# Two more unit boundaries with shared column tiles in a four-layer convolution and FFN kernel

## The chip, the cores and the metric

The kernel runs on one core of one Trainium2 chip, in one launch. The metric is device time in microseconds (us), lower being better. The kernel before was timed in three runs: 342.99, 343.20 and 343.58 us, median 343.2. One more execution was recorded by the hardware profiler; its own time was 343.52 us.

## What is computed

The reference applies two kinds of block in turn, A, B, A, B, to a sequence of 2048 tokens of 512 channels, all tensors in bf16. Block A (`_A_ref`) shifts k by a four-tap filter, multiplies it by v, convolves the product along the sequence with a filter as long as the sequence (by FFT), adds a direct term and multiplies by the normalised q. Block B is a gated feed-forward network (FFN) with 1792 hidden columns:

```python
x = A_q
x = x + _A_ref(_layernorm(x), A_k, A_v, A_shift_k, A_ssm_k, A_ssm_D)
x = x + _B_ref(_layernorm(x), B_w_gate, B_w_up, B_w_down)
x = x + _A_ref(_layernorm(x), A_k, A_v, A_shift_k, A_ssm_k, A_ssm_D)
x = x + _B_ref(_layernorm(x), B_w_gate, B_w_up, B_w_down)

def _B_ref(x, w_gate, w_up, w_down):
    return (silu(x @ w_gate) * (x @ w_up)) @ w_down
```

The convolution in A depends on k, v and the two filters only, so both A layers use the same one; the kernel computes it once.

## The kernel before

**Tiling.** The sequence is cut into four blocks of 512 tokens (index c), each held as 128 partitions by 4 rows. A block is worked on in two halves (index h) of two rows, that is 256 tokens. A *unit* is (layer, c, h): the FFN of one layer for one half. There are 16 units, and the order of `UNITS` (L946) is block by block, layer 0 then layer 1, half 0 then half 1: ... (1,1,0), (1,1,1), (0,2,0), (0,2,1), (1,2,0), (1,2,1), ..., (1,3,1).

**The convolution.** Each block's k·v and filter piece are transformed by matmuls with cosine and sine tables (lines 443, 470 and 544, all of which issue through `mm` at L323 or at L470), multiplied on VectorE (`product`, L639), and transformed back (`inverse`, L693, or for block 0 `inverse_half`, L795). ScalarE empties the matmuls' PSUM banks at L431 and L703. This work for block c+2 is spread among the FFN units of block c. The shift filter is done by 128-column matmuls with diagonal weights (`shift_mul`, L509) or, for blocks 2 and 3, by scaled copies on ScalarE (L616) and DMA transposes.

**Before a unit.** `prologue` (L894) normalises x on VectorE or ScalarE, multiplies by the convolution's result, adds, normalises again into `z` (L879 or L874), and has a DMA on SyncE's queue (SP) transpose each of the two rows of z into a slot of `zT` (L908). There are three `zT` slots; the transposed tile is what the gate and up matmuls stream.

**A unit.** `ffn` (L1003) splits the 14 column tiles of 128 hidden columns into groups, normally of 4, 4, 4 and 2. For each group `gate_up` (L949) fills PSUM banks `pf` (four of them) with gate and up products: two column tiles of 256 tokens fill a bank of 512 columns, with four matmuls of 256 streamed columns for each tile. ScalarE turns them into `sg` (silu, L974) and `ht` (L977), VectorE multiplies the two (L979), and `down` (L982) accumulates into two `pd` banks by matmuls of 512 columns. ScalarE and VectorE add the sums to x (L1075, L1078), and in layer 1 a store on SP's queue writes the row out (L1086).

**Shared column tiles.** `SHARE` (L54) names units whose last two column tiles are computed together with the next unit's (L1023 to L1027). In such a group the streamed operand is two `zT` slots at once:

```python
lo, hi = sorted(z.slot for z in zs)
return zall.t[:, lo:hi + 1:hi - lo, kd]
```

One column tile of two units then fills a bank of 512 columns: four matmuls of 512 streamed columns where there were eight of 256. The products for the next unit are kept and used when that unit comes (`left`, L1023). A shared group can only start when the next unit's `zT` has landed. Before, three boundaries are shared, after units (1,0,1), (0,2,0) and (1,3,0).

**The last unit.** For (1,3,1) the second row's down sums are split into columns 0 to `TAIL` and `TAIL` to 512 (L986, L1016). The first part goes through VectorE (L1049) and a store on SP, the second through ScalarE (L1052) and a store on ScalarE's queue (L1055). `TAIL` is 320. The first row goes out at L1039 and L1044.

**The order of the work.** Every operation is recorded with `plan.add`. The list `ORDER` gives one rank per operation, and each engine gets its operations in the order of rank (`Plan.order`, L190). Nothing is reordered afterwards: each engine runs its list, and SP and ScalarE issue DMAs in theirs. `Plan.issue` (L220) also puts *warming* matmuls on a constant tile (L1307) where its own estimates leave TensorE idle in the first 32 us; line 228 says how many. There are 25 before the four small transposes of the filter taps (L1173), 5 between them and the first transposes of the filter (`hn`, L489), and 2 more near 22 us.

Of the kernel before, what the change touches and what calls it, by code (L numbers as in the profile page):

```python
# [32 lines left out]
X0 = 'direct'  # L33
# [5 lines left out]
XVE = "AAAAAAAA"  # L39
# [12 lines left out]
TAIL = 320  # L52
VE_D = False
SHARE = {(1, 0, 1): 2, (0, 2, 0): 2, (1, 3, 0): 2}  # L54
ORDER = [
# [85 lines left out]
class Plan:  # L141
# [78 lines left out]
    def issue(self, seq, place, when, warm_until, warm):  # L220
        t, busy = 0.0, {}
# [1119 lines left out]
```

## Time and profile before

| What | Value |
|---|---|
| Median of three runs | 343.2 us (342.99 to 343.58) |
| Profiled execution's own time | 343.52 us |
| Its span | 341.7 us |
| TensorE busy | 337.7 us, 99% of the span |
| VectorE busy | 282.4 us, 83% |
| ScalarE busy | 252.5 us, 74% |
| GpSimd busy | 37.0 us, 11% |
| Mean DMA rate | 67 GB/s |
| Granted TensorE clock, mean | 0.999 |

The span is from the core's first to its last profiled instruction. PE is TensorE's matmuls and PEld its weight loads, which overlap the matmuls; DVE is VectorE, ACT ScalarE, POOL GpSimd, SP SyncE; a trailing q (SPq, ACTq) means the engine's sequencer, which waits or issues DMAs. In rows of groups, "out<-in" are the kernel's tile names, then the partitions and columns, the count, busy time in us and the mean duration of one in ns. The matmuls are pipelined: the duration of one (379 ns at 512 columns) is longer than the distance between two starts.

### The profile page before, as it was taken

The numbers are of one execution on the slowest core, as the hardware profiler recorded it, in microseconds if no ns is written. First come the engines' busy times: TensorE is split into PE (matmuls) and PEld (weight loads), VectorE is DVE, ScalarE is ACT, GpSimd is POOL, SyncE is SP. The second block draws the span as 40 slices with busy tenths as digits, with TensorE's granted clock in tenths as the row PEclk, the third lists the DMA queues.
The fourth block names the chain that finished last, engine by engine and source line by source line (L and its number), as shares of the span: only waits on it lengthen the run. The fifth ranks groups of instructions, "written<-read, shape, count | busy, mean of one in ns | idle before, by whom it ended". The sixth has DMA issues, their size and how long they took to land.

```text
span 341.7 us, 6468 instructions
## 1 busy us (share of the span) xinstructions
PE 337.7 (99%) x2563; PEld 243.7 (71%) x2563; DVE 282.4 (83%) x478; ACT 252.5 (74%) x496; POOL 37.0 (11%) x46
## 2 busy tenths in 40 slices
PE   9999999999999999999999999999999999999996
PEld 7656868768686567868587756868685877777683
DVE  7899999999999999999999999889997533726022
ACT  6899999999978475778999973869675545545451
POOL 4010100102105100103110100101101000001000
PEclk9999999999999999999999999999999999999999
DMA  7999314050215155010100224010101110001001
GB/s 287 326 293 359 59 27 67 0 155 1 34 38 102 31 96 169 2 31 2 33 19 14 48 42 129 0 33 1 33 0 39 39 36 0 16 17 28 20 33 31
DMA packets 42088, 22.95 MB, mean 67 GB/s; under 512 B 33989, under 2 KB 39882, under 8 KB 42058
## 3 DMA queue, kind: packets, MB, share of 16 engines
q1 hardware_dynamic: 41904, 22.49, 26.0%
q8 instruction: 20, 0.33, 0.4%
q14 instruction: 10, 0.08, 0.1%
q10 hardware_dynamic: 154, 0.05, 0.1%
HBM read 12.33 MB, written 2.10 MB: 42 GB/s over the span
## 4 chain that ended last, share of the span: by engine, by line
PE 96%; ACT 3%; issue 0%; ACTq 0%
PE pf L323 57%; PE pd L994 28%; PE ps L323 6%; PE ps L470 2%; ACT H L431 1%; PE wm L1307 1%; PE pt L489 1%; ACT Yk L729 1%; ACT ks L526 0%; ACT n L874 0%; PE pt L378 0%; ACT zT L940 0%; ACT X L431 0%; ACT xc L1052 0%; PE pt L1173 0%
## 5 line engine op out<-in xcount | busy, mean ns | idle before, releaser
L323 PE MATMUL pf<-zT,wg_sb 128*128 128x256 bf16 (+1 forms) x872 | 110.3, 275 | 0.0
L323 PE MATMUL pf<-zT,wu_sb 128*128 128x256 bf16 (+1 forms) x872 | 110.0, 275 | 0.1
L994 PE MATMUL pd<-wd_sb,ht 128*128 128x512 bf16 (+1 forms) x462 | 106.2, 373 | 0.0
L323 PEld LDWEIGHTS <-wu_sb 128*128 128x128 bf16 x872 | 85.3, 98 | 18.9 <-issue 0.6
L323 PEld LDWEIGHTS <-wg_sb 128*128 128x128 bf16 x872 | 85.3, 98 | 17.4
L977 ACT CAST ht<-pf 128x512 bf16<-128x512 f32 x112 | 64.7, 589 | 23.3 <-PE pf L323 22.9
L974 ACT ACTIVATE sg<-pf 128x512 bf16<-128x512 f32 x112 | 66.3, 603 | 20.8 <-PE pf L323 17.3
L994 PEld LDWEIGHTS <-ht 128*128 128x128 bf16 x462 | 45.0, 98 | 44.1
L979 DVE TENSOR_TENSOR ht<-ht,sg 128x1024 bf16<-128x1024 bf16 (+1 forms) x61 | 38.8, 640 | 19.9 <-ACT ht L977 13.8
L826 POOL TENSOR_TENSOR rstd<-ve,nhalf 128x2 f32<-128x2 f32 x24 | 25.0, 1045 | 192.7 <-DVE ve L824 192.7
L821 DVE BATCH_NORM_STATS2 bnst<-xc 128x6 f32<-128x512 bf16 x48 | 31.8, 684 | 0.5
L1075 ACT CAST dn<-pd 128x512 bf16<-128x512 f32 x30 | 17.3, 590 | 17.5 <-PE pd L994 17.5
L431 ACT ACTIVATE X<-ps 128x512 bf16<-128x512 f32 x32 | 19.0, 607 | 10.5 <-PE ps L323 10.0
L1078 DVE TENSOR_TENSOR xc<-xc,dn 128x1024 bf16<-128x1024 bf16 x15 | 10.3, 686 | 16.8 <-ACT dn L1075 16.8
L669 DVE TENSOR_TENSOR t<-X,G 128x2048 bf16<-128x2048 bf16 x18 | 21.9, 1216 | 0.1
L665 DVE TENSOR_TENSOR t<-X,G 128x2048 bf16<-128x2048 bf16 x18 | 21.9, 1217 | 0.0
L855 POOL TENSOR_TENSOR rstd<-ve,nhalf 128x2 f32<-128x2 f32 x8 | 8.4, 1044 | 79.6 <-ACT ve L853 79.6
L679 DVE TENSOR_TENSOR Z<-Z,t 128x2048 bf16<-128x2048 bf16 x12 | 14.7, 1221 | 0.3
L677 DVE TENSOR_TENSOR t<-t,t 128x2048 bf16<-128x2048 bf16 x12 | 14.6, 1219 | 0.2
L431 ACT ACTIVATE H<-ps 128x512 bf16<-128x512 f32 x24 | 14.1, 611 | 0.0
L901 DVE TENSOR_TENSOR n<-n,Yk 128x1024 bf16<-128x1024 bf16 x15 | 10.3, 689 | 3.2 <-ACT n L874 1.9
L323 PE MATMUL ps<-hs,fwd 128*128 128x512 bf16 x40 | 12.7, 379 | 0.1
(103 smaller groups left out, 322.4 us busy)
## 6 DMA issues: line engine op xcount, KB each, us to landing
hn<-in_A_ssm_k_dram SPq DMA_DIRECT2D x4, 512.0 KB, 5.4
vt<-in_A_v_dram SPq DMA_DIRECT2D x4, 512.0 KB, 5.2
xc<-in_A_q_dram SPq DMA_DIRECT2D x4, 512.0 KB, 4.7
out_dram<-xc SPq DMA_DIRECT2D x15, 128.0 KB, 1.8
wg_sb<-in_B_w_gate_dram SPq DMA_DIRECT2D x1, 1792.0 KB
wu_sb<-in_B_w_up_dram SPq DMA_DIRECT2D x1, 1792.0 KB, 8.2
wd_sb<-in_B_w_down_dram SPq DMA_DIRECT2D x1, 1280.0 KB, 11.9
kn<-in_A_k_dram SPq DMA_DIRECT2D x1, 512.0 KB, 4.5
```

The costliest lines, as they stand in the source:

```text
L323: nc.tensor.matmul(o, lhsT=lhsT, rhs=rhs, start=(n == 0), stop=(n == len(terms) - 1))
L431: add("ACT", act(D), lambda: nc.scalar.activation(out=view(), in_=ps.t[:], func=ACT.Copy, scale=scale), r=[ps], w=[(buf, keys)], conv=conv)
L665: dve(n * D, lambda t1=t1, part=part: nc.vector.tensor_mul(out=t1.t[:], in0=x.t[:, sl, 0, :], in1=g.t[:, sl, part, :]), [(x, key(slots, (0 ...
L669: dve(n * D, lambda t2=t2, part=part: nc.vector.tensor_mul(out=t2.t[:], in0=x.t[:, sl, 1, :], in1=g.t[:, sl, 1 - part, :]), [(x, key(slots ...
L679: dve(n * D, lambda t1=t1, part=part: nc.vector.tensor_add(out=z.t[:, sl, part, :], in0=z.t[:, sl, part, :], in1=t1.t[:]), [t1], [zk], con ...
L821: add("DVE", 0.6, lambda st=st, i=i: nc.vector.bn_stats(out=st.t[:], in_=xs[c].t[:, i, :]), r=[(xs[c], (i,))], w=[st])
L826: add("POOL", pw, lambda: nc.gpsimd.tensor_tensor(out=rstd.t[:], in0=ve.t[:], in1=nhalf.t[:].to_broadcast((P, n)), op=ALU.pow), r=[ve, nha ...
L974: add("ACT", act(D), lambda ps=ps, sl=sl: nc.scalar.activation(out=sg.t[:, sl], in_=ps.t[:], func=ACT.Silu), r=[ps], w=[(sg, (b,))], due=( ...
L977: add("ACT", act(D), lambda ps=ps, sl=sl: nc.scalar.copy(out=ht.t[:, sl], in_=ps.t[:]), r=[ps], w=[(ht, (b,))], due=(us[0], at, 1.5, "a"))
L979: dve(n * m * W, lambda: nc.vector.tensor_mul(out=ht.t[:], in0=ht.t[:], in1=sg.t[:]), [sg], [ht], due=(us[0], (k + n) / NF, 0.0, "h"))
L994: nc.tensor.matmul((pds[o] if not cs.start else pds[HP]).t[:, cs], lhsT=ht.t[:, q, at, o * P:(o + 1) * P], rhs=wt["d"].t[:, ft, cs], start ...
L1075: add("ACT", act(D), lambda o=o: nc.scalar.copy(out=dn.t[:, o, :], in_=pds[o].t[:]), r=[pds[o]], w=[(dn, (o,))], due=(unit, 1.0, 3.0, "h"))
```

## The change

- `SHARE` gets two more entries: units (1,1,1) and (1,2,0). The boundary after (1,1,1) is one between blocks 1 and 2 and between layers 1 and 0. Unit (0,2,0) now takes over two shared column tiles and passes on two.
- `TAIL` goes from 320 to 384: the last row is stored as 384 columns by way of VectorE and SP and 128 by way of ScalarE.
- The count of warming matmuls in line 228 becomes 27 before the tap transposes and 3 after them; the 2 near 22 us stay.
- `ORDER` is another list. Up to about 100 us of the profiled execution each engine has its old sequence, but for three places: near 12 us ScalarE takes the squares of one row (L845) ahead of the sum of the next (L840) and not behind it, near 26.5 us one inverse matmul of block 0 (L809) stands ahead of 16 shift matmuls (L519) and not behind them, and near 82 us one multiplication at L979 stands ahead of a row's statistics (L821). From there on the sequences of TensorE, VectorE, ScalarE and SP differ in many places. On SP, stores, the loads of blocks 3 and the transposes stand in another order; at the end one L1086 store stands between the L1044 store and the L1055 store.
- A branch `X0 == "mix"` is added; `X0` is 'direct' in both kernels, so it is not taken.

The program for TensorE is 32 matmuls and 32 weight loads shorter, VectorE's has one multiplication at L979 less, and the other engines have the same operations as before.

```diff
-TAIL = 320
+TAIL = 384
-SHARE = {(1, 0, 1): 2, (0, 2, 0): 2, (1, 3, 0): 2}
+SHARE = {(1, 0, 1): 2, (0, 2, 0): 2, (1, 3, 0): 2, (1, 1, 1): 2, (1, 2, 0): 2}
 ORDER = [
...
-    97, 98, 58, 59, 99, 101, 61, 76, 22, 23, 25, 47, 33, 24, 70, 55, 54, 29, 32, 62, 42, 57, 68, 38, 63, 28, 53, 43, 44, 45, 46, 56, 65, 48, 51, 141,
+    97, 98, 58, 59, 99, 101, 61, 78, 22, 23, 25, 47, 33, 24, 70, 55, 54, 29, 32, 62, 42, 57, 68, 38, 63, 28, 53, 43, 44, 45, 46, 56, 65, 48, 51, 141,
...
-                            n = int((start - t - (0.35 if 0.0 < t < 8.0 else 0.3)) / 0.106)
+                            n = int((start - t - (0.3 if t > 8.0 else 0.5 if t > 0.0 else 0.1)) / 0.106)
...
+        elif X0 == "mix":
+            evx = spectrum("evx")
+            X[0] = spectrum("X0")
+            direct(vt[0], X[0], "pf", eng(XVE[:4]), (0, 2))
...
-        if X0 == "half":
+        if X0 in ("half", "mix"):
```

108 rows, old and new, of the table ORDER are left out of this document.

## The prediction

> **What bounds the kernel now.** I read the page first, then the busy time of each engine by stage, then the groups with their shapes kept apart, then the chain of waits, then the timeline at both ends. From the page, and from the table by stage:
>
> ```profile
> span 341.7 us, 6468 instructions
> PE 337.7 (99%) x2563; PEld 243.7 (71%) x2563; DVE 282.4 (83%) x478; ACT 252.5 (74%) x496; POOL 37.0 (11%) x46
> ```
>
> ```profile
> 0.00:6.40 6.40, 5.58 (x53) 5.17 (x54) 4.73 (x20) 3.78 (x7) 3.19 (x14) 1.00 0.71 254
> 6.40:33.00 26.60, 26.36 (x246) 16.94 (x245) 24.88 (x53) 24.88 (x53) 2.31 (x3) 1.00 1.07 331
> 33.00:165.00 132.00, 132.00 (x984) 96.14 (x983) 129.62 (x208) 111.12 (x223) 19.48 (x16) 1.00 0.27 55
> 165.00:338.70 173.70, 173.70 (x1287) 125.43 (x1284) 122.94 (x199) 112.41 (x215) 12.04 (x14) 1.00 0.12 29
> ```
>
> The columns after the stretch are its length, then busy time (and count) of PE, PEld, DVE, ACT and POOL, granted clock, DMA share, GB/s. From 33 to 338.7 us TensorE is busy for 132.00 of 132.00 and 173.70 of 173.70 us: it waits for nobody. So in nine tenths of the run a new order has no wait to remove; it can only add one. The time falls there only if TensorE's own work gets shorter. What is not solid TensorE work lies in the first 33 us and in the 3 us after its last matmul.
>
> **The shared column tiles.** How much shorter is the work? A busy row cannot say, since matmuls overlap; the chain of waits gives stretches without a gap (start, length, what):
>
> ```profile
> 285.62 10.48 PE pf L323 x96
> 296.11 6.04 PE pd L994 x28
> ```
>
> 96 gate and up matmuls of 256 columns in 10.48 us are 109.2 ns each, 28 down matmuls of 512 columns in 6.04 us are 215.7 ns each. Two of 256 cost 218.3, one of 512 costs 215.7: a pair saves 2.6 ns. That the wide form in `gate_up` costs the same as in `down` is in the groups, where both last 379 ns:
>
> ```profile
> L994 PE MATMUL pd<-wd_sb,ht 128*128 128x512 bf16 x434 | 103.0, 379 | 0.0
> L323 PE MATMUL pf<-zT,wu_sb 128*128 128x512 bf16 x24 | 6.0, 379 | 0.0
> ```
>
> A boundary shares 2 column tiles, each with gate and up, each of 4 contraction steps: 16 pairs. Two boundaries are 32 pairs, 32 x 2.6 ns = 0.08 us. The 32 weight loads that go save nothing more: they lie beside the matmuls (PEld 125.43 against PE 173.70). Nor does the DVE multiplication that goes: two of 512 columns become one of 1024 on an engine with 50 us idle in that stage. Sum so far -0.08 us, with ends 0 and -0.10 (the rounding of the two lengths).
>
> **The warming matmuls.** The first 7 us of TensorE, and eight later transposes with their follower:
>
> ```profile
> 0.76 2.82 PE L1307 MATMUL wm<-const-bfloat16-1.0 128*128 128x128 bf16 x25 [0.76 <-PEq L1325]
> 3.52 0.28 PE L1173 MATMUL pt<-ident,tapR 4*128 4x4 bf16 x4
> 3.73 0.72 PE L1307 MATMUL wm<-const-bfloat16-1.0 128*128 128x128 bf16 x5
> 4.50 1.86 PE L489 MATMUL pt<-ident,hn 128*128 128x128 bf16 x16
> 6.17 0.96 PE L378 MATMUL pt<-ident,kn 128*128 128x128 bf16 x12
> ...
> 8.48 0.39 PE L323 MATMUL ps<-dg,kTb 128*128 128x128 bf16 x4
> ...
> 18.53 0.61 PE L489 MATMUL pt<-ident,hn 128*128 128x128 bf16 x8
> 18.98 1.03 PE L470 MATMUL ps<-vt,fwd 128*128 128x512 bf16 x4
> ```
>
> 16 hn transposes take 6.17 - 4.50 = 1.67 us, 104 ns each; later, 8 take 0.45 us, 56 ns each. The array starts at half rate and changes near 6.2 us, though the granted clock reads 1.00 throughout. The change moves two warming matmuls from behind the tap transposes to ahead of them; the total stays 30. At about 107 ns each the 27 end near 3.65, so the taps start some 0.15 us after 3.52. The first hn transpose waits for its DMA, not for TensorE:
>
> ```profile
> PEld L489 <- DMA hn<-in_A_ssm_k_dram: 0.3, 1, 0.3
> ```
>
> So 4.50 stays. The later taps delay `tapF` and the 16 diagonal tiles made from it by 0.15 us. The first of these is read at 8.48 us, behind transposes and filter matmuls without a gap. I take 0. Ends: +0.15 (all of the delay on the path) and -0.77 (the half rate ends before the hn transposes: 16 x 48 ns). The trace is nearest to 0, because the same 30 matmuls start at the same 0.76. The Trainium skill, TensorE: Matmul & The Clock Gate, Part 1, says that the array's gate looks at activity in a window of some 3.4 us that runs freely, so that the change of rate moves by about 0.5 us from run to run; by that rule the edit does nothing and both kernels scatter by an estimated 0.25 us, half of that, around the same sum. The one profile shows the change once and cannot show the scatter.
>
> **The three moves before 100 us.** ScalarE's sum and square near 12 us change places: the same instructions, with TensorE unbroken behind them until 22 us. The multiplication near 82 us runs 0.6 us earlier and the statistics later, in a stretch without a TensorE wait. Price 0 each. The inverse matmul:
>
> ```profile
> 26.28 0.38 PE L323 MATMUL ps<-hs,fwd 128*128 128x512 bf16 x1
> 26.49 0.38 PE L809 MATMUL ps<-m,inv 128*128 128x512 bf16 x1
> 26.71 1.06 PE L323 MATMUL ps<-dg,kTb 128*128 128x128 bf16 x16
> 27.60 1.03 PE L809 MATMUL ps<-m,inv 128*128 128x512 bf16 x4
> ```
>
> It now follows the one at 26.49, which reads the other half of the same `m` tile and writes the same bank, so it has nothing of its own to wait for. The 16 shift matmuls move back by 0.22 us and their evacuation with them. By 27.8 us both orders have done the same work. Ends 0 and +0.22; I take 0, as three quarters of the shift work stays where it was.
>
> **The order after 100 us.** Work is only moved, and TensorE has no wait to lose, so the end on the good side is 0. For the other end I added up the rows' durations along the changed order, each engine by its list, and asked where a TensorE instruction is ready only just in time. The same sum over the order of before gives no wait after 33 us, as the profile has it. Two kinds of place are narrow. The first is a forward transform's bank:
>
> ```profile
> L431 ACT ACTIVATE X<-ps 128x512 bf16<-128x512 f32 x32 | 19.0, 607 | 10.5 <-PE ps L323 10.0
> ```
>
> The ring `pc` has two banks. The new order has, near 116 us, two transform matmuls, 8 gate matmuls (0.87), and a third transform. It stands 0.43 + 0.87 = 1.30 us behind the first; the first bank is free after 0.38 + 0.61 = 0.99 and two hand-overs. That leaves at most 0.3 us to spare, if ScalarE goes to it at once; if another 0.6 us copy stands first, TensorE stalls for 0.3 or more. The second is a `zT` tile: a shared group reads the next unit's tile before the present unit ends. For (1,2,1), before:
>
> ```profile
> 240.29 2.50 SPq L908 DMA_TRANSPOSE zT<-z  x2
> ```
>
> ```profile
> 245.02 1.91 PE L323 MATMUL pf<-zT,wu_sb 128*128 128x256 bf16 x16
> ```
>
> ```profile
> DMA to landing us min/median/max: 2.4/2.4/4.0
> ```
>
> Its second transpose is issued 1.2 us before 242.79, so near 241.6, lands near 244.0 and is wanted at 245.0: 1.0 us to spare. By my sum the new order wants it 2.2 us earlier and issues it only 1.6 us earlier: 0.5 us to spare (an estimate). The other new boundary has about 2. SP's moved stores and loads (each issue 0.3 to 0.6 us) and the load of block 3's `kTb` (some 26 us later, wanted 10 us after it lands) stand where SP otherwise waits for z. I take 0. Ends 0 and, for a landing at the largest 4.0 instead of 2.4, 1.6 - 0.5 = +1.1 us.
>
> **The tail.**
>
> ```profile
> 337.06 0.69 DVE L1039 TENSOR_TENSOR xc<-xc,pd 128x512 bf16<-128x512 bf16 x1 [2.09 <-PE pd L994]
> 337.77 0.33 SPq L1044 DMA_DIRECT2D out_dram<-xc  x1
> 338.47 0.49 DVE L1049 TENSOR_TENSOR xc<-xc,pd 128x320 bf16<-128x320 bf16 x1 [0.73 <-PE pd L994]
> 338.80 0.32 ACT L1052 CAST xc<-pd 128x192 bf16<-128x192 f32 x1 [4.56 <-PE pd L994]
> 338.99 0.33 SPq L1055 DMA_DIRECT2D out_dram<-xc  x1
> 339.15 0.38 ACTq L1055 DMA_DIRECT2D out_dram<-xc  x1
> ```
>
> ```profile
> out_dram<-xc SPq DMA_DIRECT2D x1, 80.0 KB, 1.7
> out_dram<-xc ACTq DMA_DIRECT2D x1, 48.0 KB, 1.7
> L1075 ACT CAST dn<-pd 128x512 bf16<-128x512 f32 x30 | 17.3, 590 | 17.5 <-PE pd L994 17.5
> ```
>
> Both stores take 1.7 us to land, whatever their size, so ScalarE's (339.15 + 1.7 = 340.85) ends the work, 0.16 after SP's. ScalarE's copy at 128 columns: between 0.32 at 192 and 0.59 at 512, a column is 0.85 ns, so 64 fewer are -0.05. SP's part: its four last matmuls end 4 x 64 columns later (215.7/512 = 0.42 ns a column, +0.11), and VectorE takes 64 columns more, at (0.69 - 0.49)/192 = 1.04 ns +0.07; together +0.18. New ends 340.80 and 340.87: +0.02. The store put ahead of L1055 fits the 0.88 us in which SP waits after 338.10; without that cover it would cost its 0.33 to 0.43. I take 0; ends -0.05 and +0.43.
>
> **Sum.** -0.08 + 0 + 0 + 0 + 0 = about -0.1 us on the profiled execution's 343.5 (a span of 341.7 and 1.8 around it). That execution is 0.3 above the median of the three runs, 343.2, so I put the time at 343.1. The runs differ by 0.6 us, 0.2%, which is about what a measurement tells from no change: 342.5 to 343.9 counts as the same.
>
> **The rivals.** *The half rate ends earlier.* The gap between the 25 warming matmuls and the taps (about 3.4 to 3.52) closes. If that lets the array change before 4.5 us, the 16 hn transposes save 0.77 us, TensorE has hardly a gap from there to 33 us (26.36 of 26.60 busy), and the gain lasts: 343.1 - 0.8 = 342.3. For it: the first stretch is where time is left. Against it: the gap is 0.1 us, the 0.26 us ahead of hn stays, and 30 matmuls are 30 matmuls. Chance 0.10.
>
> *TensorE waits for a shared tile.* The (1,2,1) tile lands late. It decides once the landing is 0.5 us over the median; at 4.0 us it costs 1.1: 343.1 + 1.1 = 344.2, slower. A too tight bank hand-over would add to it in steps of 0.3. For it: 4.0 is in the trace. Against it: the median equals the smallest, 2.4, so late ones are few. Chance 0.13.
>
> *Sharing saves nothing,* because the wide matmuls that read two slots run slower than `down`'s, by the 2.6 ns: 343.2. Against it: 379 ns in both rows. Chance 0.05.
>
> **How the numbers follow.** My forecast has 0.72, its own range 342.7 to 343.5 (the spread of the runs and the small ends above). Faster takes 0.10 from the first rival and 0.02 from the forecast's edge; slower 0.11 from the second and 0.01 from the edge; the rest, 0.76, is the same. The range 342.4 to 343.9 leaves out the far halves of the two outer rivals.
>
> **What would show it.** Right: PE without a gap from 33 us to the end, 856 rows each for gate and up, 40 of them wide at 379 ns; taps near 3.65, hn still near 4.5; the last two stores landing within 0.1 us of each other. Wrong: a TensorE wait behind `zT` near 242 us or behind L431 near 116; hn transposes at 56 ns; a last store that lands clearly later after TensorE's end than 2.1 us.

## The result and the profile after

The changed kernel takes 344.16 us (median of 20 executions, 343.5 to 346.31), the kernel before 343.26 us (20 executions, 342.86 to 345.06). The ratio is 1.0027, with a 95% interval of 1.0014 to 1.0039: slower by 0.9 us, 0.27%. The prediction said 343.1 us and no change, with 343.9 as its upper end; it was wrong.

The profiled execution does not show the loss in its total. Its span is 341.7 us and its own time 343.55 us, against 341.7 and 343.52 before. The page, the table by stage (stretch, then busy time and count of PE, PEld, DVE, ACT and POOL, granted clock, DMA share, GB/s) and TensorE's waits:

```profile
PE 336.9 (99%) x2531; PEld 239.2 (70%) x2531; DVE 281.9 (83%) x477; ACT 252.1 (74%) x496; POOL 38.0 (11%) x46
```

```profile
33.00:165.00 132.00, 132.00 (x982) 95.84 (x980) 128.69 (x206) 110.81 (x222) 19.72 (x16) 1.00 0.26 55
165.00:338.70 173.70, 173.16 (x1251) 121.58 (x1249) 122.84 (x199) 112.02 (x215) 12.78 (x14) 1.00 0.13 28
```

```profile
PE pf L323 <- DMA zT<-z: 0.4, 1, 0.4
PE pt L378 <- DMA kn<-in_A_k_dram: 0.2, 1, 0.2
```

Before, the stretch from 165 us on was solid, 173.70 of 173.70. Now 0.54 us are missing from it: 0.37 in the one wait that TensorE has there, behind a `zT` tile, and 0.17 at the end, as its last matmul now ends at 338.54 and not behind 338.70. The 0.37 count from the modelled end of the matmul before; by the starts of the matmuls the wait is longer, as worked out below. The timeline of after has its place, and what stands ahead of it:

```profile
162.04 0.68 DVE L979 TENSOR_TENSOR ht<-ht,sg 128x1024 bf16<-128x1024 bf16 x1
...
163.16 1.44 POOL L826 TENSOR_TENSOR rstd<-ve,nhalf 128x2 f32<-128x2 f32 x2 [6.00 <-DVE ve L824]
...
164.63 0.23 DVE L863 SCALAR_TENSOR_TENSOR nmr<-mv,rstd 128x2 f32<-128x2 f32 x2 [0.63 <-POOL rstd L826]
...
164.94 1.52 ACT L874 ACTIVATE z<-xc,nmr,rstd 128x512 bf16<-128x512 bf16 x2 [0.61 <-DVE nmr L863]
...
165.78 2.53 SPq L908 DMA_TRANSPOSE zT<-z  x2
...
169.58 0.59 PE L323 MATMUL ps<-Z,inv 128*128 128x512 bf16 x2
170.55 1.05 PE L323 MATMUL pf<-zT,wg_sb 128*128 128x256 bf16 x8 [0.37 <-DMA zT<-z]
```

The matmul at 170.55 is the first of unit (1,1,1). It reads its own tile, in a group that is not shared. TensorE has nothing else left and would have started at 170.02, after the two inverse matmuls. So 0.53 us are lost. The same stretch before:

```profile
162.70 0.72 POOL L826 TENSOR_TENSOR rstd<-ve,nhalf 128x2 f32<-128x2 f32 x1 [5.27 <-DVE ve L824]
163.45 0.16 DVE L863 SCALAR_TENSOR_TENSOR nmr<-mv,rstd 128x2 f32<-128x2 f32 x1
163.66 0.69 DVE L979 TENSOR_TENSOR ht<-ht,sg 128x1024 bf16<-128x1024 bf16 x1
163.96 1.56 ACT L874 ACTIVATE z<-xc,nmr,rstd 128x512 bf16<-128x512 bf16 x2
164.84 2.50 SPq L908 DMA_TRANSPOSE zT<-z  x2
...
169.82 1.91 PE L323 MATMUL pf<-zT,wu_sb 128*128 128x256 bf16 x16
```

Before, the statistics came ahead of the multiplication L979, and one L826 gave one L863. After, L979 stands ahead, two L826 run one behind the other (163.16 to 164.59), and both L863 wait for the second, although the z in question needs only the first, which ended at 163.94. The second transpose was issued at 166.08 before and at 167.03 after, 0.95 us later; TensorE wants it at 169.82 and 170.02, 0.20 later. With the typical 2.44 us from issue to landing that leaves 1.30 us to spare before and 0.55 after. It should still have done. But the transposes did not take 2.44 us. From before and from after, the two of this tile:

```profile
DMA to landing us min/median/max: 2.4/2.8/3.2
```

```profile
DMA to landing us min/median/max: 2.7/3.1/3.5
```

The second took 3.19 us before, so it landed at 169.27, still 0.55 ahead of its use. It took 3.47 after and landed at 170.50, 0.48 behind 170.02; with the hand-over the wait is 0.53.

Two other things differ. At the end, the last matmuls and what follows:

```profile
338.35 0.56 DVE L1049 TENSOR_TENSOR xc<-xc,pd 128x384 bf16<-128x384 bf16 x1 [0.84 <-PE pd L994]
338.57 0.27 ACT L1052 CAST xc<-pd 128x128 bf16<-128x128 f32 x1 [4.61 <-PE pd L994]
338.87 0.40 ACTq L1055 DMA_DIRECT2D out_dram<-xc  x1
338.93 0.33 SPq L1055 DMA_DIRECT2D out_dram<-xc  x1
```

```profile
out_dram<-xc SPq DMA_DIRECT2D x1, 96.0 KB, 1.9
out_dram<-xc ACTq DMA_DIRECT2D x1, 32.0 KB, 1.7
```

SyncE's store is now the later one, and takes 1.85 us to land instead of 1.65. From the end of the last matmul on the array (its start plus 0.42 ns a column) to the end of the span are 3.31 us, against 3.13 before.

At the start, the first gate matmul begins at 32.21 us instead of 32.88:

```profile
0.76 3.04 PE L1311 MATMUL wm<-const-bfloat16-1.0 128*128 128x128 bf16 x27 [0.76 <-PEq L1329]
3.73 0.29 PE L1173 MATMUL pt<-ident,tapR 4*128 4x4 bf16 x4
3.95 0.35 PE L1311 MATMUL wm<-const-bfloat16-1.0 128*128 128x128 bf16 x3
4.35 1.07 PE L489 MATMUL pt<-ident,hn 128*128 128x128 bf16 x16
5.61 0.84 PE L378 MATMUL pt<-ident,kn 128*128 128x128 bf16 x12 [0.19 <-DMA kn<-in_A_k_dram]
```

The 16 hn transposes took 5.61 - 4.35 = 1.26 us instead of 1.67, so the array reached its full rate while they ran. In this execution the start was 0.67 us shorter, the end 0.18 longer, and between the two, from the first gate matmul to the last matmul, 306.16 us instead of 305.72, 0.44 longer. These cancel in the span. Which of the three belong to the change, and which to the one execution, the experiments tell.

### The profile page after: what moved, and what is told of

Its sections match the earlier page's. It is cut to its first block, busy times and chain, and to the rows that moved or that the text cites. A ratio compares the mean times of both kernels' runs of the same rounds, so it can differ in the third digit from the quotient of the medians.

```text
span 341.7 us, 6401 instructions
## 1 busy us (share of the span) xinstructions
PE 336.9 (99%) x2531; PEld 239.2 (70%) x2531; DVE 281.9 (83%) x477; ACT 252.1 (74%) x496; POOL 38.0 (11%) x46
## 4 chain that ended last, share of the span: by engine, by line
PE 90%; ACT 4%; DMA 2%; DVE 2%; POOL 0%; issue 0%; SPq 0%; ACTq 0%
PE pf L323 55%; PE pd L994 26%; PE ps L323 5%; PE ps L470 2%; DMA kn<-in_A_k_dram 1%; ACT H L431 1%; DMA zT<-z 1%; ACT Yk L729 1%; ACT ks L526 0%; POOL rstd L826 0%; ACT n L874 0%; DVE bnst L821 0%; DVE ht L979 0%; DVE m L552 0%; ACT ht L977 0%
## 5 line engine op out<-in xcount | busy, mean ns | idle before, releaser
L323 PE MATMUL pf<-zT,wg_sb 128*128 128x256 bf16 (+1 forms) x856 | 111.6, 278 | 0.4 <-DMA zT<-z 0.4
L994 PE MATMUL pd<-wd_sb,ht 128*128 128x512 bf16 (+2 forms) x462 | 105.6, 373 | 0.0
L323 PEld LDWEIGHTS <-wg_sb 128*128 128x128 bf16 x856 | 83.7, 98 | 19.9 <-DMA zT<-z 0.9
L323 PEld LDWEIGHTS <-wu_sb 128*128 128x128 bf16 x856 | 83.7, 98 | 19.4 <-issue 0.6
L974 ACT ACTIVATE sg<-pf 128x512 bf16<-128x512 f32 x112 | 65.5, 606 | 15.9 <-PE pf L323 15.2
L979 DVE TENSOR_TENSOR ht<-ht,sg 128x1024 bf16<-128x1024 bf16 (+1 forms) x60 | 38.7, 648 | 16.0 <-ACT ht L977 12.1
L826 POOL TENSOR_TENSOR rstd<-ve,nhalf 128x2 f32<-128x2 f32 x24 | 25.4, 1061 | 189.8 <-DVE ve L824 189.8
L821 DVE BATCH_NORM_STATS2 bnst<-xc 128x6 f32<-128x512 bf16 x48 | 31.7, 685 | 0.5
L665 DVE TENSOR_TENSOR t<-X,G 128x2048 bf16<-128x2048 bf16 x18 | 21.9, 1216 | 0.1
L669 DVE TENSOR_TENSOR t<-X,G 128x2048 bf16<-128x2048 bf16 x18 | 21.9, 1216 | 0.0
L855 POOL TENSOR_TENSOR rstd<-ve,nhalf 128x2 f32<-128x2 f32 x8 | 8.9, 1117 | 81.1 <-ACT ve L853 81.1
```

The source lines that it names most:

```text
L323: nc.tensor.matmul(o, lhsT=lhsT, rhs=rhs, start=(n == 0), stop=(n == len(terms) - 1))
L665: dve(n * D, lambda t1=t1, part=part: nc.vector.tensor_mul(out=t1.t[:], in0=x.t[:, sl, 0, :], in1=g.t[:, sl, part, :]), [(x, key(slots, (0 ...
L669: dve(n * D, lambda t2=t2, part=part: nc.vector.tensor_mul(out=t2.t[:], in0=x.t[:, sl, 1, :], in1=g.t[:, sl, 1 - part, :]), [(x, key(slots ...
L821: add("DVE", 0.6, lambda st=st, i=i: nc.vector.bn_stats(out=st.t[:], in_=xs[c].t[:, i, :]), r=[(xs[c], (i,))], w=[st])
L826: add("POOL", pw, lambda: nc.gpsimd.tensor_tensor(out=rstd.t[:], in0=ve.t[:], in1=nhalf.t[:].to_broadcast((P, n)), op=ALU.pow), r=[ve, nha ...
L974: add("ACT", act(D), lambda ps=ps, sl=sl: nc.scalar.activation(out=sg.t[:, sl], in_=ps.t[:], func=ACT.Silu), r=[ps], w=[(sg, (b,))], due=( ...
```

## The experiments

Theory 1: the late tile near 170 us is the loss. Theory 2: the loss is in the new ends, the warming matmuls or the 384-column tail. The table has all runs. "Middle" is from the first gate matmul to the last matmul, "end" from there to the end of the span, both in the profiled execution; a median is of 10 to 12 executions (20 for the changed kernel) and scatters by some 0.1 to 0.2 us; the ratio, which is not made from the medians, can differ from them by as much as 0.15% (e4). "Before" is the kernel before on the same chip.

| Run | First gate | Middle | End | Median | Before | Ratio (95%) |
|---|---|---|---|---|---|---|
| before | 32.88 | 305.72 | 3.13 | 343.26 | | |
| after | 32.21 | 306.16 | 3.31 | 344.16 | 343.26 | 1.0027 (1.0014 to 1.0039) |
| e1_tail | 32.17 | 305.70 | 3.31 | 343.37 | 343.35 | 1.0000 (0.9986 to 1.0014) |
| e2_warm | 32.99 | 305.73 | 3.14 | 343.39 | 343.35 | 1.0005 (0.9987 to 1.0024) |
| e3_order_share | 32.50 | 306.07 | 3.15 | 343.54 | 343.35 | 1.0007 (0.9993 to 1.0022) |
| e4_stats_first | 32.95 | 306.04 | 3.36 | 344.09 | 343.35 | 1.0007 (0.9993 to 1.0021) |
| e5_nmr_swap | 32.22 | 305.62 | 3.45 | 343.19 | 343.30 | 1.0003 (0.9986 to 1.0019) |
| e6_after_old_warm | 32.27 | 306.16 | 3.47 | 343.91 | 343.30 | 1.0026 (1.0013 to 1.0040) |
| e7_after_old_tail | 32.37 | 306.06 | 3.15 | 343.61 | 343.30 | 1.0008 (0.9993 to 1.0023) |
| e8_swap_old_ends | 33.00 | 305.65 | 3.13 | 343.24 | 343.30 | 1.0000 (0.9992 to 1.0009) |
| e9_scalar_fetch | 32.60 | 306.03 | 3.47 | 344.42 | 343.43 | 1.0037 (1.0018 to 1.0055) |
| e10_vector_fetch | 32.75 | 306.65 | 3.36 | 344.55 | 343.43 | 1.0040 (1.0025 to 1.0056) |
| e11_before_late_z | 33.18 | 305.78 | 3.14 | 343.42 | 343.43 | 0.9999 (0.9984 to 1.0013) |
| e12_tail448 | 33.12 | 305.67 | 3.33 | 343.64 | 343.43 | 1.0005 (0.9993 to 1.0017) |
| e13_both_fetch | 32.37 | 306.14 | 3.30 | 343.87 | 343.39 | 1.0019 (1.0009 to 1.0029) |
| e14_tail352 | 32.47 | 305.71 | 3.24 | 343.32 | 343.39 | 1.0007 (0.9992 to 1.0022) |
| e15_sync_fetch | 32.34 | 306.21 | 3.63 | 344.04 | 343.29 | 1.0018 (1.0001 to 1.0036) |

### The parts alone

e1 is the kernel before with the new tail, e2 the kernel before with the new warming line, e3 the changed kernel with both of them put back.

```diff
# e1, on the kernel before
-TAIL = 320
+TAIL = 384
# e2, on the kernel before
-n = int((start - t - (0.35 if 0.0 < t < 8.0 else 0.3)) / 0.106)
+n = int((start - t - (0.3 if t > 8.0 else 0.5 if t > 0.0 else 0.1)) / 0.106)
# e3, on the changed kernel: both edits backwards
```

> The kernel before with TAIL = 384 alone. Late-tile theory (TensorE waits for a transposed tile in the new order): no difference to before, within 0.2 us. Tail theory: the time from TensorE's last end to the end of the span grows by 0.15 us (the profile of the changed kernel has 3.33 us from the last matmul's start to the end, before has 3.18), the time by 0.15 to 0.3. Warming theory: no difference.

> The kernel before with the new line for the warming matmuls alone (27 and 3). Warming theory: the array's change of rate comes later in most runs, +0.4 to +0.9 us. Late-tile theory and tail theory: no difference, within 0.2 us; taps start near 3.7 and the hn transposes between 4.35 and 4.5, by the DMA's landing.

> The changed kernel with TAIL = 320 and the old warming line, so that the shared tiles and the new order alone are left. Late-tile theory: +0.5 to +0.8 us over before, with a TensorE wait of 0.3 to 0.8 us for zT near 170 us in the profile. Tail and warming theories: no difference to before, at most -0.1 us from the shared tiles.

e1 and e2 show no loss in the median. e2's first gate matmul comes at 32.99 us with the new warming line, e1's at 32.17 with the old one. So the early start in the profile after is not the change's. (e2's hn transposes started at 4.76 us, later than expected.) e3 has the TensorE wait near 170 us, and its middle is 0.35 us longer than before, but its median is only 0.19 above before, less than expected, where the changed kernel's was 0.9. The wait is the order's; whether it is the whole loss, these three did not tell.

### The z that comes late

e4 puts the multiplication L979 behind the statistics again, as it was before; e5 swaps the two L863, so that z's stands ahead of the one that waits for the second L826.

```diff
# e4, on the changed kernel
-R = 4
+R = 4; ORDER[857], ORDER[830], ORDER[828], ORDER[831] = 866, 863, 864, 865
# e5, on the changed kernel
-R = 4
+R = 4; ORDER[833], ORDER[910] = 876, 877
```

> The changed kernel with one VectorE multiplication (L979, near 162 us) put behind the statistics of unit (1,1,1), so that its second zT transpose is issued about 0.6 us earlier. Late-tile theory: the TensorE wait near 170 us goes, the time falls by 0.4 to 0.6 us against the changed kernel, to 343.6 to 343.8. Tail and warming theories: it stays near 344.2.

> The changed kernel with one swap on VectorE: the small L863 instruction (nmr) that unit (1,1,1)'s z is built from goes ahead of the other one, which waits for the second of GpSimd's two L826 instructions. In the changed kernel the first L826 ended at 163.94 and the second at 164.59, and both L863 followed the second. Theory 1 (a late tile): both transposes into zT are issued about 0.6 us earlier, the TensorE wait of 0.5 us near 170 us is gone, the stretch from the first gate matmul to the last matmul falls from 306.16 to 305.65, and the time falls by 0.5 us against the changed kernel, to about 343.65, a ratio to the kernel before near 1.001. Theory 2 (the time is lost in the new ends, the warming matmuls together with the 384-column tail): the wait goes but the time stays at 344.1, a ratio of 1.002 to 1.003. Theory 3 (ScalarE's instruction fetches move along with the transposes): a wait of 0.2 to 0.5 us stays, and the time is between.

e4 missed: z did not come earlier against TensorE, and the wait stayed (middle 306.04). The two L826 on GpSimd started 0.52 us earlier against TensorE but took 1.06 and 0.96 us instead of 0.78 and 0.69, which ate the gain. Why they took longer is open: only the first of them ran beside L979, and in the profile of before an L826 at 156.75 us took 0.68 beside an L979. e5 hit. Its timeline:

```profile
163.16 1.44 POOL L826 TENSOR_TENSOR rstd<-ve,nhalf 128x2 f32<-128x2 f32 x2 [6.00 <-DVE ve L824]
...
163.98 0.16 DVE L863 SCALAR_TENSOR_TENSOR nmr<-mv,rstd 128x2 f32<-128x2 f32 x1
164.25 1.51 ACT L874 ACTIVATE z<-xc,nmr,rstd 128x512 bf16<-128x512 bf16 x2
164.63 0.16 DVE L863 SCALAR_TENSOR_TENSOR nmr<-mv,rstd 128x2 f32<-128x2 f32 x1 [0.49 <-POOL rstd L826]
...
165.08 2.92 SPq L908 DMA_TRANSPOSE zT<-z  x2
...
169.59 0.38 PE L323 MATMUL ps<-Z,inv 128*128 128x512 bf16 x1
...
170.03 1.04 PE L323 MATMUL pf<-zT,wg_sb 128*128 128x256 bf16 x8
```

z starts 0.69 us earlier, the transposes are issued 0.70 earlier, and the gate matmul starts at 170.03 without a wait, at the time worked out above (one of the two inverse matmuls ahead of it is missing from this trace). The middle is 305.62, 0.54 less than the changed kernel's. The end and the start are those of the changed kernel (3.45 and 32.22, even a longer end), and yet the median is 343.19, level with before and lower than the 343.65 that theory 1 gave. Swapping two instructions of 0.16 us takes back the loss as far as the medians tell, so theory 1 holds, and theory 2 as the only cause, by which the time would have stayed at 344.1, falls. That the ends have a part in the loss while the wait is there is not excluded by this run.

### Which part goes with the wait

```diff
# e6, on the changed kernel: the old warming line (e2 backwards)
# e7, on the changed kernel
-TAIL = 384
+TAIL = 320
# e8, on the changed kernel: e5's swap, e6 and e7 together
```

> The changed kernel with the warming line of the kernel before; order, shared boundaries and the 384-column tail stay. Theory 1 (a late tile alone): the wait near 170 us stays and the time stays at 344.1. Theory 2a (the new warming matmuls cost time together with the new order): 343.5, as with both ends put back (343.54). Theory 2b (the 384-column tail is what costs, by the 0.2 us that its last store comes later): 344.0, as nothing of the tail is changed.

> The changed kernel with the 320-column tail of the kernel before; order, shared boundaries and new warming line stay. Theory 1 (a late tile alone): the wait near 170 us stays and the time stays at 344.1. Theory 2a (the new warming): 344.0. Theory 2b (the tail): the stretch behind the last matmul is 3.15 instead of 3.31, and the time falls by 0.2 us or more, to between 343.5 and 343.9.

> The changed kernel with the two L863 instructions swapped, the old warming line and the 320-column tail: what is left of the change is the order and the two shared boundaries. If the late tile, the new tail and the new warming are all that the change costs, the wait near 170 us is gone and the sharing's 0.08 us is left: 343.2 to 343.3, a ratio of 0.9995 to 1.0. If the order costs something else than the wait near 170 us, it stays at 343.5 (1.0007) or above.

The wait is in e6 and e7 (middles 306.16 and 306.06) and not in e8 (305.65). The old warming changes nothing: e6 is as slow as the changed kernel. The old tail brings 0.5 us (e7, as e3), as the tail theory had it for e7 (343.5 to 343.9). e8 keeps of the change only the order, mended, and the two shared boundaries. Its middle is 0.07 below before's, and its median is level with before.

So the runs sort as follows, each as its median less before's. Wait and 384 columns: +0.90, +0.74, +0.61 (after, e4, e6; three more below +0.99, +0.48, +0.75: e9, e13, e15). Wait and 320 columns: +0.19, +0.31 (e3, e7). No wait and 384 columns: +0.02, -0.11 (e1, e5). Neither: +0.04, -0.06 (e2, e8). The wait costs in both rows. The tail costs some 0.5 where there is a wait and nothing where there is none. The profiles give +0.4 to +0.5 for the wait and +0.2 to +0.3 for the tail in either case; why the medians do not add up like that is open, as the differences are hardly above their scatter. The tail's part is the weaker of the two: by its ratio of 1.0007 instead of its median, e4 has only +0.24 and would stand with e3 and e7.

### The wait in the order of before

```diff
# e11, on the kernel before: L979 ahead of z's L863
-R = 4
+R = 4; ORDER[833], ORDER[857] = 876, 875
```

> The kernel before, with nothing of the change, in which VectorE multiplies (L979, 0.69 us) ahead of the small L863 that unit (1,1,1)'s z waits for, instead of behind it. Both transposes into zT are issued 0.7 us later. There were 0.55 us between the second landing and TensorE's first use at 169.82. Late-tile theory: a TensorE wait of 0.1 to 0.5 us behind zT appears near 170 us in an order that had none, and the stretch from the first gate matmul to the last matmul grows from 305.72 by as much; the time rises by as much, to 343.4 to 343.8. Rival (the wait belongs to the new order, whose shared tiles leave TensorE less work to put in between): no wait, 343.3.

Just below the lower edge of what was expected. The second transpose was issued at 166.84 and landed at 170.12, the gate and up matmuls started at 170.17, about 0.04 late. The 0.55 us to spare are used up exactly and the middle is 305.78. One instruction of 0.69 us in front of z is all that the old order could bear here.

### Why the transpose lands late

In sixteen profiles (all but e15, where few landings are recorded), 352 transposes of z into `zT` can be set beside the two queues that carry instructions (q8 with 16 KB a transfer, q14 with 8 KB). 223 of them had no such transfer starting between 0.5 us ahead of their issue and 3 us behind it; they landed in 2.29 to 2.57 us, every one. 26 had one starting 1.2 to 2.25 us behind their issue; they landed in 3.16 to 4.17 us, every one. The other 103 had one starting at some other point from 0.5 us ahead to 3 us behind, and landed anywhere from 2.32 to 4.39 us. So no landing over 2.6 us is without such a transfer, but a transfer nearby does not always delay, and the bounds of 1.2 and 2.25 us are read from these same landings. A transpose close ahead on the queue is not what delays the next: 54 of the 223 were issued less than 1.4 us behind another and landed in 2.32 to 2.49 us. In the changed kernel q14 had transfers at 166.96 and 168.98, the latter 1.95 us behind the second transpose's issue. e9, e10, e13 and e15 lengthen an engine's instruction stream ahead of that place, to move its transfer.

```diff
# e9: L1099, ScalarE's first activation, 128x1, five times
-lambda: nc.scalar.activation(out=warm1.t[:], in_=nhalf.t[:], func=ACT.Silu)
+lambda: [nc.scalar.activation(out=warm1.t[:], in_=nhalf.t[:], func=ACT.Silu) for _ in range(5)]
# e10: VectorE's first L863 five times
# e13: behind operation 741 (L977 near 124 us) and 45 (L434 near 9 us)
+plan.extra = {741: lambda: [nc.scalar.activation(out=warm1.t[:], in_=nhalf.t[:], func=ACT.Silu) for _ in range(10)],
+              45: lambda: [nc.vector.memset(spare[:], 0.0) for _ in range(10)]}
# e13 and e15 also: each recorded operation, once issued, is followed by its entry in plan.extra, if it has one
# e15: behind operation 617 (L398 near 127 us), six loads into tiles that nothing reads
+plan.extra = {617: lambda: [nc.sync.dma_start(out=t[:], in_=A_ssm_D.rearrange("(o d) -> o d", o=1)[:, 0:64]) for t in spare]}
```

> The changed kernel with ScalarE's first, tiny instruction (L1099, 128x1) issued five times instead of once, at 2.9 us, where ScalarE has 0.8 us to spare. ScalarE's later instructions then stand four places further down its instruction stream, so that a transfer of the instruction queue that belongs to ScalarE comes some 3 us earlier in the schedule. In the changed kernel two such transfers, at 166.96 and 168.98, fell beside the two transposes into zT, and the second transpose took 3.47 us from issue to landing instead of 2.4. If ScalarE's fetch delays the landing: one of the two transfers stands elsewhere, the second transpose lands in 2.4 to 2.8 us, the TensorE wait near 170 us is gone, and the time is 343.3 to 343.7. If the fetch has nothing to do with it, or is not ScalarE's: landing 3.3 to 3.5, the wait of about 0.5 stays, 344.0 to 344.2.

> The changed kernel with VectorE's first L863 instruction (128x2, 0.15 us, at 46.4 us) issued five times, so that VectorE's instruction stream is four places longer from there on; that z is later by some 0.3 us, which its tile can bear. If one of the two instruction transfers beside the transposes into zT near 167 us is VectorE's and delays the landing: that transfer stands some 3 us earlier, the landing of the second transpose changes from 3.47 to below 2.9 us, and the wait near 170 us is gone (343.3 to 343.7). If not: landing 3.3 to 3.5, the wait stays, 344.0 to 344.2.

> The changed kernel with ten tiny ScalarE instructions (128x1) put behind the L977 that ends at 124.37, where ScalarE has 2.84 us to spare, and ten VectorE memsets (128x1) behind the L434 that ends at 9.46, where VectorE has 0.96 to spare. Both engines' instruction streams are ten places longer by 160 us. If the instruction transfers at 166.96 and 168.98 are theirs and delay the second transpose's landing: they come several us earlier, before 165, the second transpose lands in 2.4 to 2.8 us, and the TensorE wait near 170 us is gone. If they delay the landing but belong to other engines, they stay and the landing stays at 3.3 to 3.5. If they have nothing to do with it: they move and the landing stays at 3.3 to 3.5 with a wait of about 0.5.

> The changed kernel with six tiny loads (1x64 of bf16 each, into tiles that nothing reads) on SyncE behind the L398 load at 126.91, where SyncE has nothing else to issue until 145. SyncE's instruction stream is six places longer from there on. If the instruction transfer at 168.98 is SyncE's and delays the second transpose: it comes some 20 us earlier (six of SyncE's instructions ahead), the second transpose lands in 2.4 to 2.6 us (the first as before in 2.4 to 2.8), the TensorE wait near 170 us is gone, the stretch from the first gate matmul to the last matmul is 305.65, and the time is 343.4 to 343.7. If it stays at 169 and the landing at 3.3 to 3.5: neither shown nor excluded, as it would be another engine's. If it moves and the landing stays at 3.3 to 3.5: the transfer is not the cause.

All four missed in the point that was to decide: the transfer near 169 us stayed (169.41, 170.18, 169.12 and 169.33), and so did the wait. In the three with recorded landings the second transpose took 3.33, 3.41 and 3.46 us. What moved: the transfer at 166.96, by four places on ScalarE to 166.30 (e9) and by ten to 152.96 (e13); and in e15 the one at 177.91, to 149.10, which was therefore SyncE's. e13 shows the effect on the first transpose. From 164 to 168.6 us, the changed kernel and e13:

```profile
q1 hardware_dynamic: 741, 0.18, 23.0%
q14 instruction: 1, 0.01, 0.7%
```

```profile
q1 hardware_dynamic: 655, 0.16, 15.6%
```

```profile
DMA to landing us min/median/max: 2.3/2.9/3.5
```

With the transfer at 166.96 gone the first transpose lands in 2.33 us instead of 2.72, while the second, which still has its transfer, takes 3.46. In e9, where that transfer starts 0.12 us behind the first transpose's issue and not 1.18, the first lands in 2.43. That an instruction transfer can delay these landings is thereby shown by one transfer, moved in two runs, and by the count above. For the second transpose it is argued from the count alone: whose transfer the one at 169 is, and that the wait would go with it, was not shown.

e10 gave something else. The five L863 took 0.94 us, not 0.3 more than one, z came 0.8 us late, and TensorE waited near 52 us as well:

```profile
46.99 0.94 DVE L863 SCALAR_TENSOR_TENSOR nmr<-mv,rstd 128x2 f32<-128x2 f32 x5
...
52.74 0.49 PE L323 MATMUL pf<-zT,wg_sb 128*128 128x256 bf16 x3 [0.23 <-DMA zT<-z]
```

By the distance of the matmuls that wait is 0.39 us, and the middle of 306.65 holds both. The tile that "can bear" 0.3 us did not bear 0.8.

### The tail

```diff
# e12 and e14, on the kernel before
-TAIL = 320
+TAIL = 448   # e12
+TAIL = 352   # e14
```

> The kernel before with the last row stored as 448 and 64 columns, twice the step of the change (320 to 384 to 448). With 384 the stretch behind the last matmul grew from 3.13 to 3.31 in the profile (SyncE's store issued 0.56 instead of 0.39 us behind it), while the median moved by less than 0.1. If SyncE's store ends the work: it is issued near 0.73 and lands near 2.58, the stretch is 3.48, and the time rises by 0.35 against before, to 343.65. If the end is not set there: 343.3, although the store comes later.

> The kernel before with the last row stored as 352 and 160 columns. By the rows at 320, 384 and 448 SyncE's store is issued 0.475 and ScalarE's 0.525 us behind the last matmul, 0.05 apart. If each store lands some 1.69 us after its issue whatever the other does: the last lands near 2.22 and the stretch behind the last matmul is 3.11, as short as with 320. If two stores issued within 0.1 us delay each other, as at 384: one lands 1.75 to 2.0 after its issue and the stretch is 3.2 to 3.4. The median stays within 0.2 us of before in both.

The last stores of e12 and of e14:

```profile
out_dram<-xc SPq DMA_DIRECT2D x1, 112.0 KB, 1.7
out_dram<-xc ACTq DMA_DIRECT2D x1, 16.0 KB, 1.5
```

```profile
out_dram<-xc SPq DMA_DIRECT2D x1, 88.0 KB, 1.7
out_dram<-xc ACTq DMA_DIRECT2D x1, 40.0 KB, 1.8
```

In e12 SyncE's store is issued 0.74 us behind the last matmul, as expected, but the end is 3.33, no longer than with 384, because the stores are 0.29 us apart and SyncE's lands in 1.69; its median is 0.21 above before, within the scatter (1.0005). In e14 they are 0.05 apart, the later one lands in 1.80, and the end is 3.24 instead of 3.11. With 384 columns they are 0.06 apart, and over eight profiles (after, e1, e4, e5, e6, e9, e10, e13) they land in 1.75 to 2.00, the last 2.41 to 2.50 us behind the last matmul; with 320 they are 0.16 apart, land in 1.65 to 1.69, and the last comes at 2.23 to 2.24. So where two stores are issued within 0.06 us, one or both land some 0.1 to 0.3 us later. By the rows at 320 and 448 that goes with the distance between them; their sizes changed along with it, and stores of one size at two distances were not run. That, and not the later issue, is what 384 columns cost in the profile: SyncE's store, issued at 0.56 and landing in 1.65, would have ended at 2.21, as early as with 320.

No run beat the kernel before by what a measurement can tell; the best, e5 and e8, are level with it.

## Why the prediction was wrong

**The shared column tiles: right.** The prediction's -0.08 is -0.07 to -0.10 in the middle (e5 305.62 and e8 305.65 against 305.72 before; e1, e2, e12 and e14, with before's order, have 305.67 to 305.73). The 40 wide matmuls each are there at 379 ns. That duration has a modelled end and settles less than the prediction makes of it. The distance between two starts does: 215.9 ns for the wide ones in the profile after, 218.4 for a pair of narrow ones. So the rival that sharing saves nothing falls.

```profile
L323 PE MATMUL pf<-zT,wu_sb 128*128 128x512 bf16 x40 | 10.1, 379 | 0.0
L323 PE MATMUL pf<-zT,wg_sb 128*128 128x512 bf16 x40 | 10.1, 379 | 0.0
```

**The warming matmuls: right that they cost nothing.** The taps start at 3.73 us (3.65 predicted), and e2 and e6 show no effect of the line. That hn stays near 4.5 was too firm: it starts between 4.31 and 4.76 with either line. The first gate matmul falls anywhere from 32.17 to 33.18 us over the sixteen profiles of kernels other than before. That spread is all there when the first kn transpose starts, at 5.58 to 6.58 us; from there to the first gate matmul it is 26.59 to 26.83 us in all of them. The rule that the prediction took from the Trainium skill, TensorE: Matmul & The Clock Gate, Part 1, that the change of rate scatters from run to run, agrees with that. The estimate of 0.25 us that the prediction worked out from it was too small for a spread of 1.0, part of which is the start of hn. The rival that the half rate ends earlier looked true in the profile after (hn in 1.26 us) and was not the change: e1 has the same with the old warming line.

**The moves before 100 us: right.** TensorE is busy for 132.00 of 132.00 us from 33 to 165.

**The order after 100 us: the step that failed.** "I take 0" is +0.4 to +0.6 (middles of 306.03 to 306.21 with the one wait, against 305.62 and 305.65). The mechanism was named, "TensorE waits for a shared tile", with 344.2 as its time, and the number is right by accident: the tile is the wrong one. The two narrow places did hold. The (1,2,1) tile landed with 0.75 us to spare, and the bank near 116 us made no wait. What failed is twofold. First, only the tiles of the new boundaries were looked at, while the new order also brought a tile with no part in the sharing, (1,1,1)'s, from 1.30 down to 0.55 us to spare, by leaving its L863 behind one that waits for another row. Second, "the median equals the smallest, 2.4, so late ones are few" treated late landings as chance that may hit any tile. All that took over 2.6 us sit beside instruction transfers, and this very tile landed in 3.19 us in the profile of before. With that in place of 2.44, the 0.55 us to spare in the new order are a wait of 0.20.

**The tail: wrong by a term.** "Both stores take 1.7 us to land, whatever their size" holds from 48 to 112 KB (the 16 KB of e12 landed in 1.47), but not for two stores issued together. The sum gave +0.02; the profiles have +0.17 to +0.34 (e15, with six loads more to wait for, left aside). In the median it is nothing on the order of before (e1) and some 0.5 beside the wait (e7 against after), which stays unexplained and is hardly above the scatter. The L1086 store put ahead of L1055 cost nothing, as predicted: L1055 was issued 0.562 us behind the last matmul with it and without it (after and e1).

**The sum.** On before's 343.3 the profiles' terms give -0.08 + 0.5 + 0.25 = 344.0 for the changed kernel, and 344.16 was measured.

## What to carry to other kernels

When an engine without a gap is given another order, the price can be set by the tile with the least time to spare, wherever it is, as here, so list that time for every tile that the order moves, with each one's own time to landing and not the median's. A small instruction that waits for someone else's result holds up whatever stands behind it on its engine: here a 0.16 us instruction in the wrong place cost 0.5 us of TensorE. And compare two profiles by stretches between fixed events, since 0.67 us of chance at the start hid 0.62 us of real loss in two equal spans.

## What the runs showed of the hardware

- A transfer of instructions (8 or 16 KB) starting 1.2 to 2.25 us behind a DMA transpose's issue went with a landing at 3.16 to 4.17 us in 26 of 26 cases, against 2.29 to 2.57 in 223 of 223 without one near; 103 with one at another distance landed in 2.32 to 4.39. Where these transfers fall depends on the program: ten more ScalarE instructions moved one by 14 us (e13), six more on SyncE moved one by 29 (e15).
- Two stores from two queues issued 0.05 to 0.06 us apart landed in 1.68 to 2.00 us (32 to 96 KB), 0.16 apart in 1.65 to 1.69 (48 and 80 KB), 0.29 apart in 1.47 and 1.69 (16 and 112 KB).
- GpSimd's L826 on 128x2 took 0.69 us with VectorE idle beside it (before, 264.22 us), 0.68 beside L979 (156.75) and 1.53 beside L665 and L669 (170.22). The Trainium skill, GPSIMD Engine Reference, 1. Specifications, says that GpSimd shares its SBUF interfaces with VectorE and contends with instructions that have two SBUF inputs. All three of these lines have two; the 1.53 agrees with that, the 0.68 shows no contention.
